# U half of the first projection as seven block products in batches 2 to 7, ahead of V, with the order drawn anew

## The chip, the cores and the metric

One Trainium2 chip, of which one core works. Its engines are TensorE (PE; the weight loads are shown as PEld), VectorE (DVE), ScalarE (ACT), GpSimd (POOL) and SyncE (SP, which here issues all DMAs). The metric is the device time of one execution in microseconds (us); lower is better.

## What is computed

Eight batches of 576 tokens. First attention: 8 heads of width 64, where heads 0 to 3 see a causal window of 32 tokens and heads 4 to 7 see every 32nd earlier token. Its output `x` (576 x 512 per batch) goes into a gated feed-forward block:

```
h = max(x @ w_in, 0);  u, v = h[:, :512], h[:, 512:]
v_n = (v - mean(v)) / sqrt(var(v) + 1e-6)          # over the 512 columns
v_s = w_spatial @ v_n + b_spatial[:, None]         # over the 576 tokens
out = (u * v_s) @ w_out
```

All is float32. A product of two float32 matrices is made as three matmuls in the format `float32r`: each operand is split into a high part and a rest, and high x high, high x rest and rest x high are added in PSUM.

## The kernel before

A batch's `x` lies transposed in four tiles `x[128 features, 2 parts, 576 tokens]`, one per pair of heads (`t` counts the pairs over all batches, four per batch; pairs 0 and 1 of a batch are local, 2 and 3 strided). Four stages follow each other on TensorE:

- **attention** of a pair: scores (L507 or L650), softmax on DVE, ACT and POOL, and the product with the values into PSUM `po` (L617 or L720). `evac_x` writes the high part of `x` (ACT, L434) and the rest (DVE, L422) straight from PSUM.
- **`moe_1`**: V, four tiles of 128 tokens, each 12 matmuls of 512 columns (L957), followed by relu out of PSUM (L915) and the normalisation (`chain`: L920 to L940) and the split into `vn` (L412 or L414, and L422). Then U, transposed, as eight groups of 12 matmuls of 288 columns (L999), each with a relu out of PSUM (ACT, L1013). The last 64 tokens of V are made in `moe_tail`, for two batches at once from batch 2 on.
- **`moe_2`**, first half: the product with `w_spatial` (L1079, and L1091 and L1092 for the tail and the bias), eight groups, each multiplied into `u` on DVE (L1101).
- **`moe_2`**, second half: the product with `w_out` (L1168), already as seven block products instead of eight (Strassen's scheme in Winograd's form): sums of blocks of `u*v_s` on DVE and POOL (`combine`, L825), splits (`parts`), and the blocks' results put together by DVE (`plus`, L1196) on their way out of PSUM. The output goes to HBM from the tiles `o` and `vv` (L1189).

Rings of buffers tie the stages: `r_x` (8 tiles of x), `r_vn` (one, used in turn for `vn` and for the sums of the second projection), `r_vv` (two, for V tiles and for the snapshots `s1` of the second projection), `r_g`, `r_u` (two each), `r_pm` (four PSUM banks).

The order of the work is set by a list scheduler, `Program.order`: every operation has a key (its priority), the engines that may do it with a price each, and its dependencies. It hands out operations engine by engine in modelled time; where two engines may do an operation, it takes the one that would end first by its prices. The keys come from the place of the stage (`plan`, `starts`, `due`) and from the table `KEYS`. Each engine then runs its instructions strictly in that order and waits with semaphores. `fillers` adds matmuls on zeros (L1349) where the schedule leaves TensorE idle early on.

## Time and profile before

| what | value |
|---|---|
| runs | 518.72 us median of 3 (517.84 to 520.33) |
| the profiled execution | 519.78 us, span 517.7 us |
| mean granted TensorE clock | 0.980 |
| busy: PE, DVE, ACT, POOL | 499.6, 363.0, 267.4, 129.0 us |
| U of one batch (L999), 96 matmuls | 12.79 us |
| longest wait of TensorE | 4.28 us, at 62.9 us, for `wsp_sb` |

The span runs from the first instruction to the last; the execution's own time is about 2 us longer. The four compute engines run side by side, so a busy engine matters only where another one waits for it. The page cuts the span into 40 slices of 12.9 us.

### The profile page before, as it was taken

Reading aid. Unit: us, or ns where it says so; the run is one execution under the profiler, and the core shown is the slowest. Engines: PE = TensorE matmul, PEld = TensorE weight load, DVE = VectorE, ACT = ScalarE, POOL = GpSimd, SP = SyncE. Lnnn points to the kernel's source line nnn. Section 1 sums busy time; section 2 is a strip of 40 time slices with the busy share of each in tenths; the row PEclk is TensorE's granted clock in tenths of the full one; section 3 lists DMA queues with packets and bytes.
Section 4 is the critical chain, followed back from the end, with each engine's and each line's share of the span. In section 5 each row is a group of like instructions: output and inputs, shape, how many; then the busy total and the mean of one; then the engine's idle time right before and its main releaser. Section 6 shows DMA issues by size and latency. Waiting matters only on the chain.

```text
span 517.7 us, 14663 instructions
## 1 busy us (share of the span) xinstructions
PE 499.6 (97%) x5884; PEld 459.3 (89%) x5884; DVE 363.0 (70%) x1093; ACT 267.4 (52%) x825; POOL 129.0 (25%) x245
## 2 busy tenths in 40 slices
PE   6779889999999999999999999999999999999997
PEld 3558779979999899998999899998999889998997
DVE  2899989969479747896369764897457861676156
ACT  5786765568554476456336276366446252233222
POOL 3355864043212121312102111233102120102000
PEclk9689979999999999999999999999999999999999
DMA  8897323454024322262023422063011300020002
GB/s 274 307 343 268 125 83 90 149 164 151 2 79 151 118 79 81 85 180 84 11 69 121 148 80 80 1 209 113 1 56 53 123 1 1 1 80 13 1 1 91
DMA packets 26243, 52.65 MB, mean 102 GB/s; under 512 B 3136, under 2 KB 11584, under 8 KB 26176
## 3 DMA queue, kind: packets, MB, share of 16 engines
q1 hardware_dynamic: 26176, 51.72, 30.3%
q8 instruction: 46, 0.75, 0.6%
q14 instruction: 21, 0.17, 0.1%
HBM read 42.27 MB, written 9.44 MB: 100 GB/s over the span
## 4 chain that ended last, share of the span: by engine, by line
PE 89%; DVE 4%; DMA 2%; ACT 2%; SPq 1%; POOL 1%; issue 1%; POOLq 0%
PE m L1079 20%; PE m L957 18%; PE m L1168 18%; PE m L999 18%; PE po L720 4%; PE po L617 3%; PE s L507 3%; PE s L650 2%; PE m L1091 2%; PE m L1092 2%; DMA k<-kT 1%; SPq L442 1%; DMA x<-wsp 1%; PE po L1349 1%; DVE w_in_sb L422 0%
## 5 line engine op out<-in xcount | busy, mean ns | idle before, releaser
L1079 PE MATMUL m<-wsp_sb,vn 128*128 128x288 f32 x768 | 113.3, 300 | 4.3 <-DVE wsp_sb L422 4.3
L1079 PEld LDWEIGHTS m<-wsp_sb,vn 128*128 128x128 f32 x768 | 107.3, 192 | 5.4 <-DVE wsp_sb L422 4.6
L999 PE MATMUL m<-x,w_in_sb 128*128 128x288 f32 x768 | 105.3, 297 | 0.0
L999 PEld LDWEIGHTS m<-x,w_in_sb 128*128 128x128 f32 x768 | 103.4, 188 | 1.2
L957 PE MATMUL m<-w_in_sb,x 128*128 128x512 f32 (+1 forms) x408 | 99.5, 399 | 0.0
L957 PEld LDWEIGHTS m<-w_in_sb,x 128*128 128x128 f32 (+1 forms) x408 | 74.5, 186 | 19.0 <-DVE x L422 0.2
L1168 PE MATMUL m<-g,w_out_sb 128*128 128x288 f32 x384 | 56.9, 298 | 0.0
L414 POOL TENSOR_SCALAR ptl<-pc 32x64 f32<-32x64 f32 (+3 forms) x89 | 37.9, 426 | 64.7 <-DVE pc L588 24.2
L1168 PEld LDWEIGHTS m<-g,w_out_sb 128*128 128x128 f32 x384 | 52.3, 188 | 1.0 <-ACT vv L434 0.3
L422 DVE TENSOR_TENSOR x<-po,x 128x288 fp32r<-128x288 f32 x64 | 27.6, 447 | 36.3 <-ACT x L434 35.6
L1101 DVE TENSOR_TENSOR u<-m,u 128x288 f32<-128x288 f32 x64 | 28.1, 453 | 30.9 <-PE m L1092 30.7
L564 ACT ACTIVATE pl<-pl,ml 128x64 f32<-128x64 f32 (+1 forms) x140 | 47.0, 339 | 4.7 <-DVE ml L544 4.3
L915 ACT ACTIVATE vv<-m 128x512 f32<-128x512 f32 (+1 forms) x37 | 22.0, 596 | 45.7 <-PE m L957 39.6
L412 ACT CAST g<-u 128x288 fp32r<-128x288 f32 x46 | 19.2, 434 | 50.2 <-DVE u L1101 49.0
L933 POOL TENSOR_TENSOR bn<-bn,sel 128x1 f32<-128x1 f32 (+1 forms) x37 | 21.1, 575 | 95.0 <-DVE bn L928 77.0
L1013 ACT ACTIVATE u<-m 128x288 f32<-128x288 f32 x64 | 25.7, 408 | 35.0 <-PE m L999 34.6
L1168 PE MATMUL m<-vn,w_out_sb 128*128 128x288 f32 x288 | 42.6, 297 | 0.0
L920 DVE BATCH_NORM_STATS2 bn<-vv 128x6 f32<-128x512 f32 (+1 forms) x37 | 25.3, 683 | 21.0 <-ACT vv L915 20.5
L1168 PEld LDWEIGHTS m<-vn,w_out_sb 128*128 128x128 f32 x288 | 39.5, 188 | 0.4
L434 ACT CAST x<-po 128x288 fp32r<-128x288 f32 x64 | 24.7, 397 | 26.2 <-PE po L617 14.4
L412 ACT COPY ptl<-pc 32x64 f32<-32x64 f32 (+3 forms) x103 | 35.7, 346 | 4.7 <-DVE pc L588 2.6
L422 DVE TENSOR_TENSOR g<-u,g 128x288 fp32r<-128x288 f32 x64 | 27.0, 449 | 7.9 <-ACT g L412 6.2
(131 smaller groups left out, 726.6 us busy)
## 6 DMA issues: line engine op xcount, KB each, us to landing
q<-qT SPq DMA_DIRECT2D x30, 295.0 KB, 4.2
outT<-o SPq DMA_DIRECT2D x48, 144.0 KB, 2.7
v_raw<-vs SPq DMA_DIRECT2D x13, 512.0 KB, 4.2
v_raw<-vl SPq DMA_DIRECT2D x16, 384.0 KB, 3.7
k<-kT SPq DMA_DIRECT2D x16, 304.0 KB, 4.5
kbd<-ks SPq DMA_DIRECT2D x32, 144.0 KB, 4.6
outT<-vv SPq DMA_DIRECT2D x16, 144.0 KB, 3.7
vn<-w_in SPq DMA_DIRECT2D x4, 512.0 KB, 4.5
```

The lines of the kernel that those rows point to most:

```text
L412: eng.copy(dst(), src())
L414: eng.tensor_scalar(dst(), src(), 1.0, 0.0, op0=ALU.mult, op1=ALU.add)
L422: eng.tensor_tensor(dst(), src(), f32(hi()), op=ALU.subtract)
L434: eng.copy(dst(), src())
L564: eng.activation(p_sb()[:m, u, :], src, AF.Exp, bias=st()[:m, u : u + 1], scale=SCALE if masked else -1.0, **total,)
L920: lambda eng: eng.bn_stats(bn()[:m, 0:6], v()[:m]), [(v,)], [(bn,)],
L957: eng.matmul(v_ps()[:m, :], x_at(kt)[:, a, :], w_in_sb[:, w, kt, HF:], start=(n == 0 and i == 0), stop=(n == NT - 1 and i == 2),)
L999: eng.matmul(u_ps()[:, :HS], w_in_sb[:, w, kt, f * P : (f + 1) * P], xs[NHP * b + kt]()[:, a, r], start=(n == 0 and i == 0), stop=(n == NT ...
L1013: lambda eng, u=u, f=f, u_ps=u_ps: eng.activation(u()[:, f * HS : (f + 1) * HS], u_ps()[:, :HS], AF.Relu),
L1079: eng.matmul(s_ps()[:, :HS], vn()[:, a, kt, fs], wsp_sb[:, w, kt, r], start=(kt == 0 and i == 0), stop=False,)
L1101: lambda eng, ug=ug, s_ps=s_ps: eng.tensor_tensor(ug(), s_ps()[:, :HS], ug(), op=ALU.mult),
L1168: eng.matmul(o_ps()[:, :HS], w_out_sb()[:, b_at, w, kk, a * P : (a + 1) * P], at(j, kk), start=first and kk == 0 and i == 0, stop=kk == 1 ...
```

## The change

**U in batches 2 to 7** (`moe_u`) is made as seven block products. `x` of a batch is cut in two halves of features (pairs 0 and 1, pairs 2 and 3) and two halves of tokens (288 each), the U half of `w_in` in 2 x 2 blocks of 256 x 256. Each product is 12 matmuls of 128 x 128 by 288 columns (two output tiles, two tiles of features, three matmuls for the parts), L1134 of the changed kernel. Before the products come four sums of x blocks (t1 to t4, two tiles each), made in place in float32, and their splits; four pieces are copied out of PSUM as snapshots or first results, and ten additions (L1145) put the rest together. The relu of U leaves the copy out of PSUM and goes into the multiplication by `v_s` (`scalar_tensor_tensor`, L1325).

**x** of these batches is written out of PSUM once, in float32 (`raws`), and split from there by `split_x`, over 576 columns. The `raws` stand in buffers that only the first batches use (`q1`, `k1`, halves of two `x1` tiles). `r_q`, `r_k`, `r_v` and `r_x` are each cut in two rings; from batch 2 on, one buffer of q, k and values and four x tiles are left.

**Sums of weights** (`block_weights`): s1 to s4 are made once after `moe_1` of batch 1, and stand in place of a block of `w_in` that is no longer read (s1), in `v_raw1` (s2) and in two `x1` tiles (s3, s4).

**Order**: in these batches U comes ahead of V in `moe_1`. The table `KEYS` has new numbers throughout, new keys for the first eight pairs' loads (`lq`, `lw`) and for the first memsets (`set`), and the filler's limits are in it (`w`).

```diff
-    "ls": (3541.9, 11770.0, 12130.5, 1637.8, 8461.5,),
+    "ls": (8504.2, 25952.5, 6448.5, 2672.9, 15921.1,),
+    "w": (65.6, 11.83, 0,),
-WARM_END, WARM_GAP, WARM_COST, WARM_COLS, WARM_SHARE = 110000.0, 700.0, 427.0, 256, 0.8
+U_COST = 11.2
+WARM_COST, WARM_COLS = 427.0, 256
...
-    r_q = Ring(sb, "q", [P, SP], F32, 2)
+    r_q = [Ring(sb, f"q{i}", [P, SP], F32, 1) for i in range(2)]
...
-    r_x = Ring(sb, "x", [P, 2, S], F32R, 8)
+    r_x = [Ring(sb, f"x{i}", [P, 2, S], F32R, NHP) for i in range(2)]
...
+    def split_x(t, due, x_t):
+        val, rin = raws[t], [(raws[t], c) for c in range(2)]
+        rnd(due - 0.7, S, lambda: x_t()[:, 0, :], val, rin, [(x_t, 0)])
+        rest(
+            due - 0.5, S, lambda: x_t()[:, 1, :], val, lambda: x_t()[:, 0, :],
+            [*rin, (x_t, 0)], [(x_t, 1)],
+        )
...
+    def block_weights(key):
+        n = HF // 2
+        for kk in range(2):
...
+                combine(at, n, made[name][1], in0, in1, op, reads, [tok(name)])
+            for name in ("s2", "s1", "s3", "s4"):
...
+                parts(at, n, made[name][1], dst, [tok(name)], to)
...
+    def moe_u(b, key):
+        side, more = r_vn.new(), r_g.new()
...
+        for kk in range(2):
+            lo, hi = xt(0, kk), xt(1, kk)
+            t1, t2, t3, t4 = col(lo, 0), col(hi, 1), col(lo, 1), col(hi, 0)
+            make(0, kk, t1, t3, t1, xin(lo), xin(lo)[:1])
+            make(2, kk, t3, t2, t3, xin(hi), xin(lo)[1:])
+            make(1, kk, t2, t2, t1, xin(lo)[:1], [*xin(hi), at_2])
+            make(3, kk, t4, t4, t2, [at_2, *xin(hi)], [at_4])
+            split(4, "t2", kk, t2, [at_2, *xin(hi)])
+            split(5, "t1", kk, t1, xin(lo)[:1])
+            split(6, "t3", kk, t3, xin(lo)[1:])
+            split(7, "t4", kk, t4, [at_4, *xin(hi)])
...
+        for a in range(2):
+            product("a11", (0, 0), alpha[a], a, t, True)
+            evac(t, HS, snap(a), lambda a=a: alpha[a]()[:, :HS], [(alpha[a],)], [(s1[a],)])
+        for a in range(2):
+            product("a12", (1, 0), alpha[a], a, t, False)
+            evac(t, HS, to(0, a), lambda a=a: alpha[a]()[:, :HS], [(alpha[a],)], [(uu[0], a)])
...
     def moe_1(b, key):
+        if b >= LEAD:
+            moe_u(b, key)
+            key += U_COST
...
+        if b >= LEAD:
+            return
         for hf in range(2):
             u = us[b, hf] = r_u.new()
...
+                    if b < LEAD:
+                        eng.tensor_tensor(ug(), s_ps()[:, :HS], ug(), op=ALU.mult)
+                    else:
+                        eng.scalar_tensor_tensor(
+                            ug(), ug(), 0.0, s_ps()[:, :HS], op0=ALU.max, op1=ALU.mult
+                        )
```

Three places of the built order follow. A row is one instruction or several equal ones (xN): line, operation, output <- inputs, shape of the output.

TensorE in the last batch, ahead of the product with `w_spatial`. Before, the last two of U's 32 rows (`m_6913`) stand ahead of it, and the last rows of V are 32 rows further up; `vn` is V normalised:

```order
L999 MATMUL m_6913<-x_6255,w_in_sb 128x288 x3
L999 MATMUL m_6913<-x_6399,w_in_sb 128x288 x3
L1079 MATMUL m_6927<-wsp_sb,vn_6761 128x288 x12
L1091 MATMUL m_6927<-wt_h,tail_6458 128x288
L1092 MATMUL m_6927<-wt_b,tail_b_74 128x288
```

In the change the last V tile (`m_7052`, L1022) stands there:

```order
L1022 MATMUL m_7052<-w_in_sb,x_26_6520 128x512 x3
L1300 MATMUL m_7070<-wsp_sb,vn_7035 128x288 x3
L1022 MATMUL m_7052<-w_in_sb,x_27_6530 128x512 x3
L1300 MATMUL m_7070<-wsp_sb,vn_7035 128x288 x3
L1300 MATMUL m_7085<-wsp_sb,vn_7035 128x288 x6
L1300 MATMUL m_7095<-wsp_sb,vn_7035 128x288 x6
L1300 MATMUL m_7103<-wsp_sb,vn_7035 128x288 x3
L1300 MATMUL m_7070<-wsp_sb,vn_7035 128x288 x3
L1300 MATMUL m_7085<-wsp_sb,vn_7035 128x288 x3
L1300 MATMUL m_7095<-wsp_sb,vn_7035 128x288 x3
L1300 MATMUL m_7103<-wsp_sb,vn_7035 128x288 x6
L1300 MATMUL m_7070<-wsp_sb,vn_7035 128x288 x3
```

U's 96 matmuls no longer stand between V and the product with `w_spatial`; the groups of that product are begun with the V tiles 0 to 2, in pieces of three, and the last row shown is the first that needs V tile 3.

TensorE in the change, from the end of the second projection of batch 6 (`m_6758` to `m_6813`, L1392) to U of batch 7 (`m_6879` and `m_6890` are a11 and a12 of the two output tiles, `m_6901` and `m_6910` s2*t2); before, V of batch 7 stood in place of the rows of L1134:

```order
L1392 MATMUL m_6777<-g_6762,w_out_sb_682 128x288 x6
L1392 MATMUL m_6813<-g_6785,w_out_sb_682 128x288 x6
L1134 MATMUL m_6879<-x_24_6505,w_in_sb 128x288 x3
L1134 MATMUL m_6879<-x_25_6512,w_in_sb 128x288 x3
L1134 MATMUL m_6890<-x_24_6505,w_in_sb 128x288 x3
L1134 MATMUL m_6890<-x_25_6512,w_in_sb 128x288 x3
L1134 MATMUL m_6901<-vn_6838,v_raw_2_1777 128x288 x6
L1134 MATMUL m_6910<-vn_6838,v_raw_2_1777 128x288 x6
L1134 MATMUL m_6879<-x_26_6520,w_in_sb 128x288 x3
L1134 MATMUL m_6879<-x_27_6530,w_in_sb 128x288 x3
L1134 MATMUL m_6890<-x_26_6520,w_in_sb 128x288 x3
```

The snapshots of `m_6879` and `m_6890` are copied to the tiles `vv` between their first and their last rows here, and the `vv` tiles are those from which the second projection's last results go to HBM.

VectorE in the first batch, up to the last rest of `w_spatial` (`wsp_sb`). Before:

```order
L544 ISA pl_75,ml_77<-s_779,cst_sb 64x64
L544 ISA ml_77 64x1
L422 TENSOR_TENSOR w_out_sb_822<-g_736,w_out_sb_822 128x256 x2
L422 TENSOR_TENSOR wsp_sb<-x_328,wsp_sb 128x576 x2
L422 TENSOR_TENSOR wsp_sb<-x_329,wsp_sb 128x576
```

In the change:

```order
L432 TENSOR_TENSOR w_out_sb_682<-g_620,w_out_sb_682 128x256
L432 TENSOR_TENSOR vn_761<-vv_833,vn_761 128x512
L513 RECIPROCAL mx_871<-mx_871 128x16
L432 TENSOR_TENSOR w_out_sb_682<-g_620,w_out_sb_682 128x256
L518 TENSOR_TENSOR pp_69<-pp_69,mx_871 128x16x18
L432 TENSOR_TENSOR wsp_sb<-x_0_546,wsp_sb 128x576
```

The masked maxima of a second local pair (ten L544 with their read-outs) no longer stand ahead of the last `wsp_sb`; 142 instructions of VectorE come up to it before, 123 in the change, and GpSimd makes two of the four rests of `w_spatial` instead of one.

More of the change, by code (lines that the diff above doesn't have):

```diff
@@ L34 @@
 SB = STRIDE // 4
+LEAD = 2
+ALONE = LEAD * NHP
 SP = S + STRIDE - RA
@@ L321, in fillers @@
         ends, free, found = {}, 0.0, {}
+        until, least, share = KEYS["w"]
         for at, n, e in issued:
@@ L761, in attention @@
                 load(
-                    due - 33, lambda j=j: kbd[j::2, t % 2, j, STRIDE:],
+                    first + 1, lambda j=j: kbd[j::2, t % 2, j, STRIDE:],
                     ks[b, hp - 2, j], [("k", t % 2, j)], 64 * S * 4, [("k0", t % 2)],
                 )
-            load(due - 20, v, vs[b, hp - 2], [(place,)], P * 1024 * 4)
+            load(last, v, vs[b, hp - 2], [(place,)], P * 1024 * 4)
             kin = [("k", t % 2, j) for j in range(2)]
-        xs[t] = r_x.new()
+        xs[t] = r_x[b if b < LEAD else 0].new()
+        if b >= LEAD:
+            raws[t] = raw_x(t)
         (local_attention if local else strided_attention)(t, due, q, k, v, [(place,)], kin)
+        if t in raws:
+            split_x(t, due, xs[t])
     def x_tok(t):
+        if t in raws:
+            return [(xs[t], i) for i in range(2)]
         return [(xs[t], i, c0) for i in range(2) for c0 in ((0, 3) if t % NHP < 2 else (0, 1))]
@@ L1024, in keep_tails @@
                 t = NHP * b + hp
+                if i == 1:
+                    at = lambda j, hp=hp: xt()[:, hp, j, TAIL:]
+                    src = lambda t=t: raws[t]()[:, 4 * P :]
+                    rin = [(raws[t], c) for c in range(2)]
+                    rnd(key, TAIL, lambda at=at: at(0), src, rin, [(xt, hp, 1, 0)], (POOL, ACT))
+                    rest(
+                        key, TAIL, lambda at=at: at(1), src, lambda at=at: at(0),
+                        [*rin, (xt, hp, 1, 0)], [(xt, hp, 1)],
+                    )
+                    continue
                 rnd(
@@ L1314, in attention_moe @@
         add(
-            -90, [(DVE, 250), (POOL, 400)],
+            KEYS["set"][1 + h], [(DVE, 250), (POOL, 260)],
             lambda eng, h=h: (
@@ L1344, in attention_moe @@
         (moe_tail, moe_1, moe_2)[kind](b, k0)
+        if kind == 1 and b == lead - 1 and nb > lead:
+            late.extend(raw_slots())
+            block_weights(k0 + cost[1])
     ctx.enter_context(tc.manual_schedule())
```

221 lines of the change are left out of this document (179 added, 42 removed), and 4 rows, old and new, of the table KEYS.

## Prediction

> **What bounds the kernel now.** I read the page first: busy times, slices, chain.
>
> ```profile
> span 517.7 us, 14663 instructions
> PE 499.6 (97%) x5884; PEld 459.3 (89%) x5884; DVE 363.0 (70%) x1093; ACT 267.4 (52%) x825; POOL 129.0 (25%) x245
> PE   6779889999999999999999999999999999999997
> PEclk9689979999999999999999999999999999999999
> PE 89%; DVE 4%; DMA 2%; ACT 2%; SPq 1%; POOL 1%; issue 1%; POOLq 0%
> ```
>
> TensorE carries the chain. Only the first six slices (78 us) hold digits below 9 and a lowered clock. The windows say how full the rest is, and what the other engines have left there:
>
> ```profile
> 70.00:130.00 60.00, 60.00 (x877) 55.02 (x877) 53.22 (x182) 38.83 (x130) 21.52 (x40) 0.98 0.39 120
> 170.00:290.00 120.00, 119.96 (x1519) 112.32 (x1520) 86.48 (x279) 63.42 (x206) 24.20 (x52) 1.00 0.32 99
> 100.00:510.00 410.00, 409.96 (x4664) 382.93 (x4663) 274.82 (x852) 200.15 (x624) 78.97 (x166) 1.00 0.24 76
> ```
>
> From 100 to 510 us TensorE is without work for 0.04 us. In the 120 us from 170, about the work of two batches, DVE has 33.5 us free, ACT 56.6 and POOL 95.8. So a matmul less is time less there, unless something new makes TensorE wait. The chain of waits gives the price of U, as the last batch shows:
>
> ```profile
> 464.16 11.20 PE m L957 x48
> 475.36 12.80 PE m L999 x96
> 488.15 1.58 PE m L1079 x12
> ```
>
> V, U and the product with w_spatial stand without a gap, and one matmul of U takes 12.80/96 = 133.3 ns. In the head, the timeline of TensorE:
>
> ```profile
> 62.64 0.29 PE L1079 MATMUL m<-wsp_sb,vn 128*128 128x288 f32 x1
> 67.21 7.99 PE L1079 MATMUL m<-wsp_sb,vn 128*128 128x288 f32 x42 [4.28 <-DVE wsp_sb L422]
> ```
>
> The load in the chain, and DVE's timeline:
>
> ```profile
> 53.05 4.08 DMA x<-wsp
> ```
>
> ```profile
> 63.92 0.21 DVE L544 CUSTOM_DVE_ANT_0 pl<-s,cst_sb 128x64 f32<-128x64 f32 x1
> ...
> 65.08 0.74 DVE L422 TENSOR_TENSOR w_out_sb<-g,w_out_sb 128x256 fp32r<-128x256 f32 x2
> 65.75 2.08 DVE L422 TENSOR_TENSOR wsp_sb<-x,wsp_sb 128x576 fp32r<-128x576 f32 x3
> ```
>
> The windows after the stop (PE busy, granted clock, DMA share):
>
> ```profile
> 67.20:72.00 4.80, 4.79 (x20) 0.50 0.29 107
> 72.00:77.00 5.00, 5.00 (x59) 0.99 0.02 5
> ```
>
> TensorE stands for 4.28 us, because the rests of w_spatial are last in a DVE queue: the load had landed by 57.13. After the stop it runs 4.80 us at a granted clock of 0.50, which costs another 2.4. This stop is worth 4.3 + 2.4 = 6.7 us.
>
> **The matmuls taken away.** Seven products of 12 instead of eight make 84 matmuls for 96, the same shape, in six batches: 72 x 133.3 ns = **-9.6 us**, all on the bounding engine. The chip cannot hide this term; only new waits can eat it.
>
> **The added elementwise work.** Its prices, from the groups by shape:
>
> ```profile
> L1013 ACT ACTIVATE u<-m 128x288 f32<-128x288 f32 x64 | 25.7, 408 | 35.0 <-PE m L999 34.6
> L434 ACT CAST x<-po 128x288 fp32r<-128x288 f32 x64 | 24.7, 397 | 26.2 <-PE po L617 14.4 <-PE po L720 9.9
> L422 DVE TENSOR_TENSOR x<-po,x 128x288 fp32r<-128x288 f32 x64 | 27.6, 447 | 36.3 <-ACT x L434 35.6
> L412 ACT CAST g<-u 128x288 fp32r<-128x288 f32 x46 | 19.2, 434 | 50.2 <-DVE u L1101 49.0 <-DVE o L825 0.4 <-DVE w_out_sb L422 0.2
> L422 DVE TENSOR_TENSOR g<-u,g 128x288 fp32r<-128x288 f32 x64 | 27.0, 449 | 7.9 <-ACT g L412 6.2 <-POOL g L414 1.7
> L825 DVE TENSOR_TENSOR u<-u,u 128x288 f32<-128x288 f32 x16 | 7.2, 456 | 0.5
> L1196 DVE TENSOR_TENSOR o<-m,o 128x288 f32<-128x288 f32 x32 | 14.4, 449 | 1.4 <-PE m L1168 1.3
> L412 ACT CAST wsp_sb<-x 128x576 fp32r<-128x576 f32 x1 | 0.7, 671 | 0.0
> L422 DVE TENSOR_TENSOR wsp_sb<-x,wsp_sb 128x576 fp32r<-128x576 f32 x3 | 2.1, 740 | 0.0
> L422 DVE TENSOR_TENSOR vn<-vv,vn 128x512 fp32r<-128x512 f32 x32 | 22.5, 717 | 3.0 <-ACT vn L412 2.0 <-POOL vn L414 0.5
> L422 DVE TENSOR_TENSOR w_in_sb<-vn,w_in_sb 128x512 fp32r<-128x512 f32 x4 | 4.3, 1084 | 0.0
> L422 POOL TENSOR_TENSOR w_out_sb<-g,w_out_sb 128x256 fp32r<-128x256 f32 x4 | 3.6, 899 | 0.2
> L422 POOL TENSOR_TENSOR wsp_sb<-x,wsp_sb 128x576 fp32r<-128x576 f32 x1 | 1.7, 1745 | 0.1
> ```
>
> Per batch it removes 8 relus (8 x 0.408 = 3.3 us) and 8 pairs that write x out of PSUM (8 x 0.844 = 6.8). It adds 8 plain copies of x (3.2), 4 splits of 576 columns (4 x 1.41 = 5.6), 8 sums (3.6), 8 splits of 288 (7.1), 4 copies and 10 additions out of PSUM (1.6 + 4.5). The net is 25.6 - 10.1 = 15.5 us of DVE-speed work per batch, 31 in 120 us, against the 186 us that the three engines have free. The multiplication by v_s keeps its shape and I price its new form at nothing (ends -0.1 and +0.1 us on DVE each, a tenth more or less of the 449 ns of L1196, which also reads PSUM, in a stage that DVE does not bound).
>
> The built order puts most of it on POOL: two-input operations on arrays with both inputs in SBUF go from 10 to 194 on POOL, from 289 to 257 on DVE. The rows 899 ns (256 columns) and 1745 (576) put one of 288 at about 0.98 us, an estimate, so POOL gains 184 x 0.98 = 180 us and stands near 309 of 509. All engines stay under three quarters; the average does not bind.
>
> **Do they get in each other's way?** The rests of 512 columns took DVE 717 ns for vn and 1084 for w_in_sb, in the head, where POOL is busy: half as much again. DVE's 257 operations, at 0.45 us, fill 23% of the time; 23% of POOL's 180 us is 41 us together, and half of it, 21 us, is DVE's loss. It fits in the free 33.5 of each 120; I charge TensorE **+1.5 us**, nearer to nothing since the row of 170 to 290 leaves room; the ends are 0 and +21 (every stretched operation waited for).
>
> The Trainium skill is harder here: on its page SBUF — State Buffer, section Who interferes with whom, a DVE instruction with two SBUF inputs and a GpSimd instruction that reads SBUF cannot run at once, and the later one blocks fully. The 1084 ns agree that one delays the other; no single row shows a full block. By that rule the whole 41 us would be lost to one of the two, an estimate that the third rival below turns into a time.
>
> **The sums of weights** are made once, between V of batch 1 and U of batch 2: 4 sums of 512 and 8 of 256 columns, 8 splits of 256, about 4 x 0.72 + 8 x 0.45 + 8 x 0.88 = 13.5 us. In 70 to 130 us DVE has 6.8 us free, ACT 21.2, POOL 38.5. They fit by sum, with DVE nearly full and POOL as the cover; I take **+1.0** (ends 0 and +6.7, half of them late).
>
> **U ahead of V.** Until now U's 12.8 us covered the last V tile's normalisation. Its length, in the last batch:
>
> ```profile
> 475.39 0.60 ACT L915 ACTIVATE vv<-m 128x512 f32<-128x512 f32 x1 [1.47 <-PE m L957]
> ```
>
> ```profile
> 479.55 0.69 DVE L422 TENSOR_TENSOR vn<-vv,vn 128x512 fp32r<-128x512 f32 x1 [0.69 <-ACT vn L412]
> ```
>
> From V's end at 475.36 to 480.24 are 4.9 us, plus a signal of some 0.2. In the built order 33 matmuls stand between V's last and the first that needs that tile: 4.4 us. So TensorE waits **0.7 us** in batch 7. In batches 3 and 5 attention matmuls of the next pair stand in the gap, and in 2, 4 and 6 the tail of V, so I take nothing there; the ends are 0 and, with one queued 1.7 us POOL operation in each of the three batches, +5.8.
>
> **The snapshots' buffers.** The tile vv that a second projection stores from is now written again by U's snapshot, 4 us earlier in need than by V:
>
> ```profile
> 464.29 0.67 SPq L1189 DMA_DIRECT2D outT<-vv  x1
> ```
>
> ```profile
> outT<-vv SPq DMA_DIRECT2D x16, 144.0 KB, 3.7
> ```
>
> The last store, issued 0.1 us after the projection's end (464.16), lands by the median of 3.7 us (the issue table's last number) 3.8 after it; the copy (0.4) and a signal end at 4.4, and a12 of the second tile stands at 30 matmuls, 4.0. That is 0.4 us at worst, six times 2.4; **+0.5**, because in batches with attention its matmuls stand between.
>
> **The head.** Ahead of the last rest of w_spatial DVE has 19 instructions less: ten masked maxima (63.92 to 65.08: 1.2 us), two rests of w_in (2.2), one each of vn, wsp_sb and a sum, against some 2.5 us of others. That is about 3 us less, and POOL has two more array operations of w_in and one of w_spatial. At the same place TensorE has 1.8 us more attention to do first. Together they exceed 4.28, so the stop should close and with it the half clock: up to -6.7. Against it: POOL's rest of 1745 ns can be the last one now, and the filler matmuls are gone. I take **-4.0**, the stop without the clock; ends 0 and -6.7. Loads keep their number and bytes, and the one q and k buffer from batch 2 on costs nothing while DMA is 24% busy from 100 us.
>
> **Sum:** -9.6 + 1.5 + 1.0 + 0.7 + 0.5 - 4.0 = -9.9 us. The profiled execution took 519.78 (span 517.7): 509.9. The median of the runs is 1.06 lower: **508.8 us**.
>
> **Rivals.**
> - The head does not gain: the stop goes to another wait, a sum or a rest on POOL. DVE's last rests depend on POOL's high parts. 508.8 + 4.0 = 512.8.
> - Everything is covered and the head gains in full: 518.7 - 9.6 - 6.7 = 502.4. For it: 0.04 us of waiting in 410 now. Against it: two new waits with less cover.
> - The lock: POOL and DVE block each other and the sums reach U late. If a quarter of the 41 us reaches TensorE in place of the 1.5, 508.8 + 8.8 = 517.6, no change that can be told. For it the 1084 ns; against it that V and the product stages leave time.
> - Slower: the hand-over from V to w_spatial in batches 3, 5 and 7. If queued work makes the last tile's chain 4.3 us longer than its cover, each wait is like the one at 62.9: 4.3 and then 2.4 of half clock. That is 3 x 6.7 = 20 less the 0.7 counted: 528. It needs ten masks (1.2), a POOL operation (1.7) and 0.9 more ahead of it in all three, and batch 7 has no attention.
>
> **Chances.** Forecast 45%, head without gain 20%, all covered 15%, lock 13%, hand-over 7%. The range 502 to 517 holds the first three and some of the lock, and cuts off most of the rest. A measurement here tells about 0.5% (2.6 us) from no change. Faster than 516.1: the first three and a little of the lock, 82%; within: most of the lock, 11%; slower than 521.3: 7%.
>
> **What would show it.** 84 matmuls of 133 ns per U, 11.2 us, in place of 12.8; TensorE without a stop of 4 us before the first w_spatial product and a clock above 0.98; waits under 1 us between V and w_spatial in batch 7 and at a12; POOL near 310 us busy and DVE near 370. Wrong would be TensorE under 99% busy from 100 us on, a group of stops behind POOL, or a clock of 0.5 after 80 us.

## The result and the profile after

The changed kernel takes **546.89 us** (median of 4 runs, 545.78 to 547.54), the kernel before 518.85 (517.84 to 520.33, on the same chip): a ratio of **1.054, 95% interval 1.051 to 1.057**. It is 28 us slower, where 508.8 was forecast. The profiled execution has a span of 545.3 us. Its busy times, slices, granted clock and chain of waits:

```profile
span 545.3 us, 14749 instructions
...
PE 494.4 (91%) x5790; PEld 450.8 (83%) x5790; DVE 416.1 (76%) x1073; ACT 290.3 (53%) x886; POOL 295.6 (54%) x424
...
PE   3397969999899899999999999998998999899997
...
PEclk9989999999989999999999999999999999999999
...
PE 39%; DVE 36%; ACT 7%; DMA 7%; POOL 5%; issue 4%; SPq 1%; DVEq 0%; ACTq 0%; POOLq 0%
```

TensorE held 89% of the chain before; now VectorE holds nearly as much as TensorE. The clock is not the reason: its mean over the span is 0.991, before 0.980. To see where the time went, both runs are cut at the same two places of the work: the start of the last matmul with `wt_b` that closes the `w_spatial` stage of batch 1, and the one of batch 7. From the timeline of TensorE, before:

```profile
152.51 0.29 PE L1092 MATMUL m<-wt_b,tail_b 97*128 97x288 f32 x1
...
502.73 0.29 PE L1092 MATMUL m<-wt_b,tail_b 97*128 97x288 f32 x1
```

and after:

```profile
68.41 5.46 PE L1300 MATMUL m<-wsp_sb,vn 128*128 128x288 f32 x39
78.03 0.40 PE L1312 MATMUL m<-wt_h,tail 128*128 128x288 f32 x1 [4.16 <-DVE tail L432]
...
160.20 0.29 PE L1313 MATMUL m<-wt_b,tail_b 97*128 97x288 f32 x1
...
529.56 0.29 PE L1313 MATMUL m<-wt_b,tail_b 97*128 97x288 f32 x1
```

| stretch, us | before | after | difference |
|---|---|---|---|
| up to the last matmul of the product with `w_spatial` in batch 1 | 152.51 | 160.20 | +7.7 |
| from there to the same place in batch 7 (the six changed batches) | 350.22 | 369.36 | +19.1 |
| the rest | 14.97 | 15.74 | +0.8 |

The middle stretch should have shrunk by 9.6 us to 340.6, so 28.7 us of waiting and of broken-up work came in there. The windows of the middle stretch, and of some stages in it, before (the stretch; V and U of batch 3; its product with `w_spatial`; the second projections of batches 3 and 4 with the attention beside them):

```profile
152.64:502.86 350.22, 350.18 (x3855) 328.54 (x3853) 231.06 (x695) 161.89 (x493) 63.37 (x132) 1.00 0.22 72
237.00:257.80 20.80, 20.80 (x226) 19.30 (x225) 10.09 (x23) 9.95 (x23) 5.49 (x11) 1.00 0.01 1
257.80:272.80 15.00, 15.00 (x118) 14.99 (x113) 9.97 (x41) 4.97 (x25) 0.43 (x1) 1.00 0.22 69
272.80:288.60 15.80, 15.76 (x263) 14.82 (x262) 14.82 (x40) 10.00 (x27) 4.17 (x11) 1.00 0.52 171
336.40:352.00 15.60, 15.60 (x294) 14.89 (x281) 15.53 (x48) 9.78 (x32) 4.62 (x11) 1.00 0.59 193
```

and after (the stretch; V of batch 3; its product with `w_spatial`, now with attention beside it; the second projection of batch 4):

```profile
160.33:529.69 369.36, 348.86 (x3718) 319.09 (x3717) 281.27 (x696) 178.49 (x534) 186.29 (x268) 1.00 0.22 69
256.50:267.00 10.50, 10.50 (x47) 8.49 (x46) 5.27 (x13) 2.94 (x5) 2.75 (x5) 1.00 0.01 2
267.00:287.50 20.50, 20.38 (x309) 19.14 (x308) 19.76 (x56) 15.01 (x50) 16.82 (x22) 1.00 0.34 100
352.20:368.00 15.80, 14.86 (x270) 13.66 (x268) 14.83 (x27) 8.32 (x24) 11.57 (x16) 1.00 0.29 100
```

TensorE now stands 20.5 us of the stretch (369.36 - 348.86), in 32 stops of 0.2 to 1.9 us. The other 8.2 of the 28.7 us are longer rows. Most of them are an after-effect of the stops, by this estimate: a matmul of 288 columns has a row of 297 ns, and the next one starts 133 ns after it where the run is unbroken, so at each stop the last row runs out alone, 32 x 0.16 = 5.2 us. The third column of busy times is VectorE. Over the stretch it is busy 76%, which looks harmless; but it is 50% busy beside V (5.27 of 10.50) and 96% beside `w_spatial` and the attention that now stands there (19.76 of 20.50; 66% before, without attention). The stage of the second projection was 94 and nearly 100% full in the kernel before (14.82 of 15.80 and 15.53 of 15.60), rows that the prediction did not read; TensorE lost 0.04 us beside them. What TensorE waits for, and what the two-input operations cost, by groups (the last column is the idle time ahead and who ended it):

```profile
L1300 PE MATMUL m<-wsp_sb,vn 128*128 128x288 f32 x768 | 117.4, 303 | 4.5 <-DVE vn L432 2.2 <-DVE u L1325 0.9 <-ACT vn L422 0.9
L1392 PE MATMUL m<-vn,w_out_sb 128*128 128x288 f32 x288 | 43.7, 300 | 4.5 <-DVE vn L432 2.4 <-DVE o L1420 2.0
L1134 PE MATMUL m<-x,w_in_sb 128*128 128x288 f32 x144 | 23.6, 305 | 6.4 <-ACT vv L444 3.8 <-DVE vv L1420 2.6
L1134 PE MATMUL m<-vn,x 128*128 128x288 f32 x72 | 11.5, 295 | 0.0
L1312 PE MATMUL m<-wt_h,tail 128*128 128x288 f32 x64 | 19.2, 307 | 7.4 <-DVE tail L432 7.4
L432 DVE TENSOR_TENSOR x<-x,x 128x576 fp32r<-128x576 f32 x17 | 19.2, 1158 | 0.0
L432 DVE TENSOR_TENSOR g<-u,g 128x288 fp32r<-128x288 f32 x29 | 21.2, 746 | 0.3 <-POOL g L424 0.3
L432 POOL TENSOR_TENSOR g<-u,g 128x288 fp32r<-128x288 f32 x35 | 31.7, 912 | 14.6 <-ACT g L422 13.5 <-PE m L1392 0.5
```

A matmul of U costs what it did (295 ns against 297; 305 in the group that holds the stops). Of the 20.1 us in the 32 stops, 6.8 stand at U (snapshots and last results in `vv`), 5.6 at `w_spatial` and its tail (splits `vn`), 5.0 at the second projection (splits `vn`, sums `o`) and 2.7 at attention, in three waits for a load of values (1.02, 0.94 and 0.76 us). Two chains behind the stops at U, first a queue of VectorE and the stop that it ends, then a copy of ScalarE that waits for a store and the longest stop:

```profile
174.69 0.84 DVE L432 TENSOR_TENSOR vn<-q,vn 128x288 fp32r<-128x288 f32 x1
175.45 2.04 DVE L432 TENSOR_TENSOR vn<-x,vn 128x288 fp32r<-128x288 f32 x2
...
177.78 0.44 DVE L1420 TENSOR_TENSOR vv<-m,vv 128x288 f32<-128x288 f32 x1
178.27 1.85 PE L1134 MATMUL m<-x,w_in_sb 128*128 128x288 f32 x12 [0.94 <-DVE vv L1420]
...
375.99 0.40 ACT L444 COPY vv<-m 128x288 f32<-128x288 f32 x1 [1.55 <-DMA outT<-vv]
376.44 1.05 PE L1134 MATMUL m<-x,w_in_sb 128*128 128x288 f32 x6 [1.92 <-ACT vv L444]
```

In the first, three splits of the new sums (read from `q1` and an `x1` tile) stand ahead of the second projection's result in `vv`. In the second, the snapshot may not be written to `vv` until the store from it has landed. A rest of 288 columns takes VectorE 746 ns, before 449; one of 576 columns 1158, before 740.

### The profile page after: what moved, and what is told of

Its sections match the earlier page's. It is cut to its first block, busy times and chain, and to the rows that moved or that the text cites. A ratio compares the mean times of both kernels' runs of the same rounds, so it can differ in the third digit from the quotient of the medians.

```text
span 545.3 us, 14749 instructions
## 1 busy us (share of the span) xinstructions
PE 494.4 (91%) x5790; PEld 450.8 (83%) x5790; DVE 416.1 (76%) x1073; ACT 290.3 (53%) x886; POOL 295.6 (54%) x424
## 4 chain that ended last, share of the span: by engine, by line
PE 39%; DVE 36%; ACT 7%; DMA 7%; POOL 5%; issue 4%; SPq 1%; DVEq 0%; ACTq 0%; POOLq 0%
PE m L1022 11%; PE m L1134 8%; DVE vn L432 7%; PE m L1300 6%; PE m L1392 5%; DVE x L432 4%; ACT pl L613 3%; PE m L1210 2%; DMA outT<-vv 2%; DVE bn L985 2%; DVE vv L1005 2%; DVE o L1420 2%; DVE g L432 2%; PE po L666 2%; DMA v_raw<-vs 2%
## 5 line engine op out<-in xcount | busy, mean ns | idle before, releaser
L1300 PE MATMUL m<-wsp_sb,vn 128*128 128x288 f32 x768 | 117.4, 303 | 4.5 <-DVE vn L432 2.2
L1022 PE MATMUL m<-w_in_sb,x 128*128 128x512 f32 (+1 forms) x408 | 100.2, 400 | 0.0
L1022 PEld LDWEIGHTS m<-w_in_sb,x 128*128 128x128 f32 (+1 forms) x408 | 75.2, 187 | 18.9 <-issue 0.2
L1392 PE MATMUL m<-g,w_out_sb 128*128 128x288 f32 x384 | 57.4, 298 | 1.2 <-ACT vv L444 1.1
L1392 PEld LDWEIGHTS m<-g,w_out_sb 128*128 128x128 f32 x384 | 52.7, 188 | 2.9 <-ACT vv L444 2.2
L424 POOL TENSOR_SCALAR ptl<-pc 32x320 f32<-32x320 f32 (+3 forms) x81 | 34.9, 431 | 30.3 <-DVE pc L637 20.7
L1392 PE MATMUL m<-vn,w_out_sb 128*128 128x288 f32 x288 | 43.7, 300 | 4.5 <-DVE vn L432 2.4
L422 ACT COPY ptl<-pc 32x320 f32<-32x320 f32 (+3 forms) x111 | 38.8, 350 | 11.7 <-DVE pc L637 10.4
L1392 PEld LDWEIGHTS m<-vn,w_out_sb 128*128 128x128 f32 x288 | 39.4, 188 | 6.7 <-DVE vn L432 2.9
L985 DVE BATCH_NORM_STATS2 bn<-vv 128x6 f32<-128x512 f32 (+1 forms) x37 | 25.4, 688 | 21.7 <-ACT vv L980 21.6
L432 POOL TENSOR_TENSOR g<-u,g 128x288 fp32r<-128x288 f32 x35 | 31.7, 912 | 14.6 <-ACT g L422 13.5
L1005 DVE TENSOR_SCALAR vv<-vv,bn 128x512 f32<-128x512 f32 (+1 forms) x37 | 24.8, 670 | 14.3 <-POOL bn L998 14.3
L422 ACT CAST g<-u 128x288 fp32r<-128x288 f32 x55 | 22.5, 434 | 16.2 <-DVE u L1325 10.5
L1145 DVE TENSOR_TENSOR u<-m,vv 128x288 f32<-128x288 f32 x36 | 16.2, 451 | 19.4 <-PE m L1134 16.2
L1134 PE MATMUL m<-x,w_in_sb 128*128 128x288 f32 x144 | 23.6, 305 | 6.4 <-ACT vv L444 3.8
L1325 DVE SCALAR_TENSOR_TENSOR u<-u,m 128x288 f32<-128x288 f32 x48 | 20.3, 442 | 10.1 <-PE m L1313 10.0
L1134 PEld LDWEIGHTS m<-x,w_in_sb 128*128 128x128 f32 x144 | 19.8, 188 | 8.8 <-ACT vv L444 5.0
L1210 PE MATMUL m<-x,w_in_sb 128*128 128x288 f32 x192 | 26.5, 297 | 0.0
```

Of the source, the lines that this page charges most:

```text
L422: eng.copy(dst(), src())
L424: eng.tensor_scalar(dst(), src(), 1.0, 0.0, op0=ALU.mult, op1=ALU.add)
L432: eng.tensor_tensor(dst(), src(), f32(hi()), op=ALU.subtract)
L985: lambda eng: eng.bn_stats(bn()[:m, 0:6], v()[:m]), [(v,)], [(bn,)],
L1005: lambda eng: eng.tensor_scalar(v()[:m], v()[:m], bn()[:m, 6:7], bn()[:m, 9:10], op0=ALU.subtract, op1=ALU.mult),
L1022: eng.matmul(v_ps()[:m, :], x_at(kt)[:, a, :], w_in_sb[:, w, kt, HF:], start=(n == 0 and i == 0), stop=(n == NT - 1 and i == 2),)
```

## The experiments

The theories: **A**, the two-input work on GpSimd; **B/H**, the new place and hand-overs of U; **C**, VectorE has no room; **D**, the new table of keys; **E**, the fewer buffers; **F/G**, attention pressed into the late stages, or not; **I**, the sums of x and their splits. Each time stands beside the kernel before on the same chip, with the ratio and its 95% interval.

### Two-input work back on VectorE

One number of the table moves 185 operations:

```diff
-    "dp": (18607.0, 455.0,),
+    "dp": (18607.0, -1038.4,),
```

> The changed kernel with one number of the order's table set back: the surcharge that the planner puts on VectorE for an operation with two inputs that GpSimd could also do (dp, second number) is -1038.4 ns as before, not +455. It moves about 185 two-input operations from GpSimd to VectorE (TENSOR_TENSOR: VectorE 431 to 616, GpSimd 229 to 44); products, buffers and all other keys stay. Theory A (the lost time comes from two-input work on GpSimd, which is itself slow, 0.9 to 1.7 us, and stretches VectorE's operations): TensorE's waits fall from 47 us towards 25, the rest of vn out of u falls from 847 back to about 490 ns, and the time goes to 515 to 528 us. Theory B (the waits belong to the new place of U and its buffers, whoever does the sums): within 1.5% of 547. Theory C (VectorE has no room for that work): VectorE above 430 us busy and the time 540 or more.

Measured: **549.9 us, ratio 1.059 (1.057 to 1.062)**, no gain.

```profile
PE 496.8 (91%) x5790; PEld 454.4 (83%) x5790; DVE 434.1 (79%) x1258; ACT 272.4 (50%) x832; POOL 154.0 (28%) x293
```

GpSimd falls from 296 to 154 us, and the time does not fall with it. The middle stretch is 364.0 us, 5 better than the change, and the head 7.5 worse (batch 1 ends at 167.65). So A is not the main cause; what is taken from GpSimd fills VectorE instead (434.1 us), and both the time and VectorE lie where C put them.

### The kernel before with its work moved to GpSimd

```diff
-    "dp": (12894.8, -1038.4,),
+    "dp": (12894.8, 455.0,),
...
-    "dpt": (657.16,),
+    "dpt": (887.79,),
```

> The kernel before with that surcharge as in the change (455 ns, for the first 888 us): 109 two-input operations go from VectorE to GpSimd (TENSOR_TENSOR: VectorE 499 to 390, GpSimd 45 to 154), nothing else is changed on purpose. Theory A: slower than before by 10 to 25 us (109 of 185 moved operations, and the changed kernel lost some 37 us against its own sum), with TensorE waits after 100 us where there was 0.04. Theory B: 517 to 523 us.

Measured: **527.8 us, ratio 1.017 (1.015 to 1.020)**. Moving 109 operations to GpSimd costs 8.4 us, below A's 10 to 25, and nothing like the change's distance from its forecast, 38 us. Of the 8.4, 4.2 lie ahead of batch 2 (batch 1 ends at 156.68) and 2.1 in the middle stretch (352.3).

### The disputed price by itself

Streams of ten, each begun when the ones before are done:

```
        ("a", (("vector", tt),)),
        ("b", (("gpsimd", tt),)),
        ("c", (("vector", tt), ("gpsimd", tt))),
        ("e", (("vector", from_psum), ("gpsimd", tt))),
        ("h", (("vector", one), ("gpsimd", tt))),
```

> Not the computation: streams of ten equal operations on 128 x 288 float32, on one engine alone and on two at once, and zeros as output. It measures the disputed price: a two-input operation on VectorE (alone about 0.37 to 0.45 us) and one on GpSimd (alone 0.6 to 0.9 us), and both at once. If the two exclude each other fully, both streams at once take the sum of their lone times (about 1.3 us per pair); if they only slow each other, VectorE's takes up to 0.85 and GpSimd's stays near 0.95. With one input from PSUM, or with one input in all, VectorE should be untouched if only the second SBUF input matters.

Groups of the run: v is VectorE, g GpSimd; a and b are two-input operations alone, c both at once, d VectorE with one input from PSUM alone and e beside GpSimd, g a one-input operation of VectorE alone and h beside GpSimd.

```profile
L35 POOL TENSOR_TENSOR gc<-x,go_c 128x288 f32<-128x288 f32 x10 | 9.8, 1010 | 0.5 <-ACT go_c L70 0.5
L35 DVE TENSOR_TENSOR vc<-x,go_c 128x288 f32<-128x288 f32 x10 | 9.2, 985 | 8.6 <-ACT go_c L70 8.6
L44 DVE TENSOR_SCALAR vh<-go_h 128x288 f32<-128x288 f32 x10 | 7.6, 834 | 0.5 <-ACT go_h L70 0.5
L35 POOL TENSOR_TENSOR gb<-x,go_b 128x288 f32<-128x288 f32 x10 | 7.5, 794 | 9.4 <-ACT go_b L70 9.4
L38 DVE TENSOR_TENSOR ve<-bank,go_e 128x288 f32<-128x288 f32 x10 | 3.7, 450 | 0.5 <-ACT go_e L70 0.5
L38 DVE TENSOR_TENSOR vd<-bank,go_d 128x288 f32<-128x288 f32 x10 | 3.7, 448 | 1.1 <-ACT go_d L70 1.1
L35 DVE TENSOR_TENSOR va<-x,go_a 128x288 f32<-128x288 f32 x10 | 3.7, 447 | 0.0
L44 DVE TENSOR_SCALAR vg<-go_g 128x288 f32<-128x288 f32 x10 | 2.3, 304 | 4.3 <-ACT go_g L70 4.3
```

This is one execution. Ten of each take 3.7 and 7.5 us alone, 11.2 one after the other, and 9.8 together: of the 3.7 us that could overlap, 1.4 do. The slow-down is larger than the milder expectation (985 ns, not up to 850). One input from PSUM leaves VectorE untouched (448 and 450 ns). The Trainium skill, page "SBUF — State Buffer", section "Who interferes with whom", says that the two share one pair of ports that an instruction holds to its end; the 9.8 of 11.2 us nearly agree.

### The old U with the new keys and buffers

`moe_1` and `moe_2` as before, with no `raws`, no `moe_u` and no `block_weights`, under the table of keys and the rings of the change:

```diff
-        if b >= LEAD:
-            raws[t] = raw_x(t)
...
-        if b >= LEAD:
-            moe_u(b, key)
-            key += U_COST
```

> The changed kernel with its table of keys and its split rings, but U in the old form in all batches: eight products behind V, x written out of PSUM in two parts, no sums of x or of weights. 159 TENSOR_TENSOR are on GpSimd, 385 on VectorE. Theory A: slower than before, 528 to 540 us, since the sums of the second projection and the rests are still on GpSimd. Theory B (the new U costs the time): 519 to 525 us. Theory D (the new table of keys is bad by itself, above all in the head): 540 or more, most of the loss before 100 us.

Measured: **555.8 us, ratio 1.073 (1.066 to 1.081)**. The form without the seven products is 8.9 us slower than the change. B falls as the only cause: keys and rings lose the time even with the old U. D has the size right and the place wrong: 4.5 us of the loss lie ahead of batch 2 (batch 1 ends at 156.98) and 28.0 in the middle stretch (378.3).

### Rings alone, keys alone

The kernel before with the rings of the change, and then with its own rings and the new keys:

```diff
-    r_x = Ring(sb, "x", [P, 2, S], F32R, 8)
+    r_x = [Ring(sb, f"x{i}", [P, 2, S], F32R, NHP) for i in range(2)]
```

(and the same for q, k and values.)

> The kernel before, table of keys and all, with only the rings of the change: one q, one k and one value buffer from batch 2 on instead of two, four x tiles instead of eight; U in eight products behind V, nothing on GpSimd that was not there (TENSOR_TENSOR: VectorE 499, GpSimd 45, as before). Theory E (the four x tiles and single load buffers make attention wait for V and U of the batch before, and then TensorE wait for attention): 535 to 560 us, with waits at the attention matmuls (for loads of q, k, v or for the rests of x). Theory D (the new keys cost the time): 517 to 524 us. Theory A (GpSimd) says 517 to 524 as well, but the first four runs already spoke against it as the main cause.

> The kernel before, with its rings of two and of eight, U in eight products behind V, and only the new table of keys. Theory D: 540 us or more. Theory E: 520 to 532 us, of which up to 8.4 by the work that the new keys give to GpSimd (163 TENSOR_TENSOR; the kernel before with 154 there took 8.4 us more).

> The changed kernel, seven products ahead of V, with the table of keys of before for everything that both have (TENSOR_TENSOR: VectorE 610, GpSimd 50). Theory D: 505 to 520 us, the 9.6 us of matmuls less than before and some waits at U. Theory E: 535 to 555 us, since the buffers are those of the change.

| us | keys of before | keys of the change |
|---|---|---|
| rings of before, old U | 519.3 | 534.4, ratio 1.030 (1.028 to 1.033) |
| rings of the change, old U | 563.6, ratio 1.086 (1.082 to 1.090) | 555.8 |
| rings of the change, new U | 554.1, ratio 1.068 (1.062 to 1.074) | 546.9 |

The rings alone cost 44 us, a little more than E's range, the new keys alone 15, between the ranges of D and E, and the new U gives 9 us back in both columns. Of the keys' 15 us, 12 lie ahead of batch 2 (batch 1 ends at 164.63); the middle stretch is 350.6, as before. Of the rings' 44, the stretch up to batch 1 takes 13.4 and the middle one 32.6.

### Which rings

> The kernel before with one ring of the change: x in two rings of four tiles, of which only the first is used from batch 2 on; q, k and values keep two buffers, U stays in eight products, the keys are those of before. Theory E1 (the four x tiles are the cause: the attention of the next batch can write x only after the last product of this batch that reads it): 540 to 565 us. Theory E2 (the single load buffers are the cause): 517 to 525 us.

> The kernel before with the other rings of the change: one q, one k and one value buffer from batch 2 on, eight x tiles as before. Theory E2: 535 to 555 us, with waits of TensorE for loads of q and values. Theory E1: 518 to 530 us; some waits for loads can be there, but attention runs far enough ahead to take them.

Measured: x alone **533.8 us (1.027, 1.022 to 1.031)**, loads alone **532.9 (1.026, 1.022 to 1.029)**; neither expectation of "the one or the other" holds. The x ring costs 13.5 us in the middle stretch (363.7) and nothing in the head. The load rings cost 12.6 us in the head and 0.9 behind it (351.1). Both together cost 32.6 there: of 22.0 us of stops, 14.7 stand at attention's matmuls, 5.0 of these behind a load of q or values; with the x ring alone it was 2.1 of 7.3. That fits attention that is held back by x and has nothing fetched ahead with which to catch up. A part is the clock: behind stops the granted clock is 0.59 from 209 to 217 us in the run with the x ring (worth 3.3 us), and in the run with both 0.66 from 228 to 238, 0.57 from 366 to 370 and 0.72 from 488 to 494 (worth 6.8); in the kernel before it was 1.00 throughout the stretch. The head of the run with the load rings, where before there was no stop between 47.5 and 62.9 us:

```profile
60.94 1.19 PE L702 MATMUL s<-kbd,q 128*32 128x36 f32 x64 [7.30 <-DVE ml L593]
...
69.72 0.84 PE L1203 MATMUL m<-x,w_in_sb 128*128 128x288 f32 x2 [2.09 <-ACT w_in_sb L422]
```

Its first 100 us issue the same kinds of loads in another order. One buffer less between two requests may change what the scheduler finds ready, so that a table of keys made for one order does not fit the next; no run here shows that this is the reason.

### The new U in fewer batches

```diff
+BLOCK = 6
-        if b >= LEAD:
+        if b >= BLOCK:
             raws[t] = raw_x(t)
...
-        xs[t] = r_x[b if b < LEAD else 0].new()
+        xs[t] = r_x[b % 2 if b < BLOCK else 0].new()
```

> The new U and the new rings only in batches 6 and 7 (eight x tiles, two q, k and value buffers up to batch 5), keys of before; the sums of weights are made after V of batch 5. If the loss belongs to the buffers, it scales with the batches that run with few of them: of the some 35 to 44 us of six batches a third at most, and batch 7 has no attention behind it, so 518 to 530 us; the matmuls give back 2 x 1.6 = 3.2 us. If the new U itself (place ahead of V, snapshots, sums) costs the time, the same range holds and the waits stand at its matmuls, not at attention's.

> The same with batches 4 to 7: the loss of the buffers in three attention stages (batches 4 to 7) instead of five, 525 to 545 us, less 4 x 1.6 = 6.4 us of matmuls already in that range; linear between the two-batch and the six-batch form (554).

Measured: **543.9 us (1.047, 1.042 to 1.051)** and **547.8 (1.054, 1.050 to 1.059)**: above both ranges, and not in proportion to the batches. 19 to 20 us of it are lost up to the end of batch 0, in the head again (the product with `w_spatial` of batch 0 ends at 105 to 106 us, before 86); batches 2 to 5 of the two-batch form take what they took before, and batches 6 and 7 take 6.5 us more, in spite of 3.2 us of matmuls less.

### Attention earlier, VectorE only later, load buffers back

```diff
-    "lead": (-4.89,),
+    "lead": (10.0,),
...
+    "dp2": (12894.8, -1038.4,),
...
-            held = KEYS["dp"][locks] if now < KEYS["dpt"][0] * 1000.0 else 0.0
+            held = KEYS["dp" if now < 200000.0 else "dp2"][locks] if now < KEYS["dpt"][0] * 1000.0 else 0.0
...
-    r_q = [Ring(sb, f"q{i}", [P, SP], F32, 1) for i in range(2)]
+    r_q = [Ring(sb, "q", [P, SP], F32, 2)] * 2
...
+            name: (x_homes[1], lambda t: t.rearrange("p a s -> p (a s)")) for name in ("s2", "s3", "s4")
```

> The changed kernel with one number of the table of keys set anew: from batch 2 on attention falls due 14.9 us earlier (lead -4.89 to 10). In the built order more of attention then stands beside V and U (348 matmuls behind a V row for 196) and less in the second projection. Theory F (the buffers press the next batch's attention into the stages of w_spatial and w_out, where VectorE is then 95% busy and its sums come late): 530 to 541 us, less waiting from 160 us on. Theory G (attention cannot go earlier whatever its key, since the buffers hold it, or the sums of U are late by themselves): 544 to 552 us.

> The changed kernel with the two-input work given back to VectorE only behind 200 us of the planner's time (surcharge -1038.4 ns there, +455 ahead of it, so that the head stays as it is): 114 operations leave GpSimd. By the stage times of the first experiment (batches 3 to 7: 293 us against 301 with GpSimd) theory A in its small form says 8 us less than the change, 537 to 541 us. If that difference came from the shifted head alone, 545 to 549.

> Both numbers together. If F and A are two causes beside each other, 522 to 534 us; if both are the same full VectorE queue, no better than the better one of the two alone.

> The changed kernel with two q, k and value buffers kept in all batches. Room for them is made by leaving work out: the sums of weights s2, s3 and s4 share one tile, so their products take the same, wrong block; every instruction, its shape and its engine choice stay possible as they were. Theory E (x tiles and load buffers together hold attention): the loss behind the head falls from 34 us by about half, as in the form with the x ring alone (18.6 us lost there against 38.5 with both): 525 to 537 us. Theory G or A: 543 to 550 us.

| run | us | ratio (95%) | middle stretch |
|---|---|---|---|
| the change | 546.9 | 1.054 (1.051 to 1.057) | 369.4 |
| attention earlier | 555.4 | 1.071 (1.066 to 1.075) | 372.4 |
| VectorE only behind 200 us | 547.5 | 1.056 (1.052 to 1.061) | 370.3 |
| both | 549.7 | 1.059 (1.053 to 1.064) | 367.5 |
| two load buffers | 558.6 | 1.076 (1.066 to 1.081) | 365.7 |

None brings a gain. The earlier attention and the two load buffers end above every range given for them. VectorE behind 200 us lies in the range for a difference that came from the shifted head alone (545 to 549), and both together are no better than the better one, as the second reading says. But the 5 us of the first experiment may only be hidden here: behind stops the granted clock fell to 0.66 from 245 to 250 us and from 405 to 410 and to 0.72 from 462 to 468, worth 5.1 us, where the changed kernel kept 1.00 in the whole stretch. The two-buffer form gains 3.7 us in the stretch and loses 15 in the head. So neither the due time of attention nor the engine of the sums nor the load buffers, set anew by itself under these keys, wins the time back.

### The products alone, with the sums, with the buffers

The kernel before with its keys, and `moe_u` without sums (plain halves of x and blocks of `w_in` go into the products):

```diff
+        plain = {"t1": (0, 1), "t2": (1, 1), "t3": (0, 0), "t4": (1, 0)}
...
+                half, hf = plain.get(src, src)
```

With the sums, `moe_u` makes and splits them from x, into a ring of their own:

```diff
+        made, side, more = r_sum.new(), r_vn.new(), r_g.new()
...
+            make(0, kk, col(lo, 1), col(lo, 0), x_tok(lo))
```

With the few buffers, the changed kernel loses its sums:

```diff
-            block_weights(k0 + cost[1])
```

> The kernel before, with its keys and its buffers (eight x tiles, two q, k and value buffers), and of the change only the products: in batches 2 to 7 U is made ahead of V as seven block products with snapshots, four copies and ten additions. Left out are the sums of x and of weights: the products that need them read plain halves of x and plain blocks of w_in, so U is wrong. It costs nothing to have x written in two parts as before. Theory H (U ahead of V, its snapshots and additions cause the waits): a loss behind the head of 20 us or more, as in all forms with the new U so far (31 to 44), so 520 to 535 us. Theory E (few buffers and the sums that fill them): a loss like that of before (5 us) or up to 10, so 509 to 515 us, near the prediction without its gain in the head.

> The products alone (517.5 us) and beside them the eight sums of x per batch and their splits into vn and g, as in the change, with eight x tiles and two q, k and value buffers as before. Left out are the sums of weights (plain blocks of w_in in their place), x is summed by its high part, and s1 to s4 of w_out share one place, which makes room for the sums: U and the output are wrong, the work is there. The sums bring 8 x 0.45 + 8 x 0.88 = 10.7 us of VectorE-speed work per batch. Theory I (the sums and splits are the cause: they fill VectorE in the stages of w_spatial and w_out and use the one vn buffer twice): 530 to 545 us, waits at the sums of the second projection and at U. Theory E (few buffers): 517 to 524 us.

> The products with the buffers of the change (four x tiles, one q, k and value buffer from batch 2 on, x written once in float32 and split later), but without the sums of x and of weights (plain halves and blocks in their place, so U is wrong). Keys as in the run with the changed kernel and the old table (554.1 us), which had both, and whose head was 13 us longer than before by the load buffers. Theory E: 545 to 554 us, a loss behind the head of 25 to 34 us. Theory I: 525 to 534 us, of which some 13 in the head, and behind it at most 10 more than the products alone.

Measured: products alone **517.5 us (0.995, 0.993 to 0.997)**; with the sums **528.5 (1.017, 1.012 to 1.022)**; with the few buffers **532.4 (1.025, 1.022 to 1.028)**. The first two lie between the ranges of their two theories, the third in that of I. With the changed kernel under the old keys (554.1) they make a square: the sums cost 11.0 us with the buffers of before and 21.7 with the few. TensorE's ends of the stretch and some of its stops, products alone, with the copy of ScalarE that ends one of them:

```profile
152.90 0.29 PE L1276 MATMUL m<-wt_b,tail_b 97*128 97x288 f32 x1
...
172.63 2.67 PE L1097 MATMUL m<-x,w_in_sb 128*128 128x288 f32 x18 [0.99 <-ACT vv L444]
...
233.71 0.40 ACT L444 COPY vv<-m 128x288 f32<-128x288 f32 x1 [1.29 <-DMA outT<-vv]
234.16 6.12 PE L1097 MATMUL m<-x,w_in_sb 128*128 128x288 f32 x44 [0.84 <-ACT vv L444]
...
500.56 0.29 PE L1276 MATMUL m<-wt_b,tail_b 97*128 97x288 f32 x1
```

with the sums, with VectorE's queue ahead of one of the stops, and the later part of the second projection of batch 3 with the first 3 us of the next U (windows):

```profile
155.82 0.30 PE L1308 MATMUL m<-wt_b,tail_b 97*128 97x288 f32 x1
...
291.02 3.12 DVE L433 TENSOR_TENSOR vn<-sum,vn 128x288 fp32r<-128x288 f32 x5
294.06 0.45 DVE L1415 TENSOR_TENSOR o<-m,o 128x288 f32<-128x288 f32 x1
294.56 2.66 PE L1387 MATMUL m<-g,w_out_sb 128*128 128x288 f32 x18 [1.21 <-DVE o L1415]
...
512.18 0.29 PE L1308 MATMUL m<-wt_b,tail_b 97*128 97x288 f32 x1
```

```profile
282.80:300.00 17.20, 15.02 (x197) 13.99 (x196) 17.06 (x47) 7.93 (x26) 5.24 (x9) 1.00 0.58 191
```

with the few buffers, and then with both (the changed kernel, keys of before):

```profile
162.93 0.29 PE L1278 MATMUL m<-wt_b,tail_b 97*128 97x288 f32 x1
...
515.00 0.29 PE L1278 MATMUL m<-wt_b,tail_b 97*128 97x288 f32 x1
```

```profile
169.12 0.29 PE L1313 MATMUL m<-wt_b,tail_b 97*128 97x288 f32 x1
...
534.92 0.29 PE L1313 MATMUL m<-wt_b,tail_b 97*128 97x288 f32 x1
```

The stretch takes 347.7, 356.4, 352.1 and 365.8 us. So the way from 350.2 to the changed kernel's 369.4 goes: matmuls -9.6 (worked out); waits at the hand-overs of the products +7.0 (347.7 against 340.6); sums of x with their splits +8.7; few buffers, with x written once and split from there, +4.4; both together 5.0 more than their sum, the sums of weights in it; the new keys, GpSimd's work with them, +3.6. These are stage times of one profiled execution each, and the runs of one kernel lie up to 4.4 us from their median, so a term may be off by about that much: the 8.7 and the 7.0 stand clear of it, the other three hardly. And 1.7 of the 5.0 are the clock: the run with both stops for 2.54 us at 283.2 for a load of values, and its granted clock is 0.72 from 286 to 292, while it is 1.00 in the stretch of the other runs of this list.

In the window with the sums VectorE is busy 17.06 of 17.20 us and TensorE 15.02. In the second projection of batch 3 before, VectorE was busy 14.82 of 15.80 and TensorE 15.76; with the products alone (274 to 291 us) 16.50 of 17.00 and 16.24. So the stage had about 1 us to spare, and the splits of the sums go into it: five of them, 3.1 us, stand in VectorE's queue ahead of the result `o` for which TensorE stops at 294.56, and the same five ahead of the stops of 2.10 us at 417.35 and 1.62 at 473.51. A full VectorE does not stop TensorE by itself (15.53 of 15.60 us before, and no stop); what stands ahead of a result that TensorE needs does.

## Why the prediction was wrong

By the two profiled executions the change came out 27.6 us longer where the sum said 9.9 shorter. The 37.5 us between them are 11.7 in the head, 7.2 for the sums and splits, 5.8 for U's hand-overs, 4.4 for the few buffers, 4.0 for these together with the sums (the sums of weights in it), 3.6 for the keys in the middle stretch and 0.8 behind it. The step that failed is the one that let all new work and all waits pass nearly free: room was read off an average, and the buffers and the order drawn anew got no price.

- **The matmuls, -9.6 us:** agrees. With the same keys and rings the new U is 8.9 us faster than the old one, under the old keys 9.5 (563.6 to 554.1), and a matmul of U takes 295 ns against 297. "Only new waits can eat it" is what came.
- **The added elementwise work, +1.5 with ends 0 and +21:** mis-sized, by its room. "It fits in the free 33.5 of each 120" took the average of two batches for the room of each stage. The sums and splits cost 8.7 us on top of the products, inside the ends but far from the 1.5, and more beside the few buffers. "The average does not bind" was true and beside the point: VectorE was 94 to nearly 100% busy in the stage that had to take the splits, and 49% beside V and U (10.09 of 20.80), and the splits stand ahead of results that TensorE waits for.
- **GpSimd and VectorE in each other's way:** the collision is there, and harder than the half that was assumed (9.8 us for 11.2 us of work). But putting the work back on VectorE gained nothing, which fits one shortage of both engines better than a price of GpSimd alone. POOL was forecast near 310 us busy and came to 296; DVE near 370 and came to 416, with the rests of 288 columns at 746 ns.
- **U ahead of V, +0.7, and the snapshots' buffers, +0.5:** 7.0 in the products alone. The hand-over from V to `w_spatial` in batch 7 was there and smaller than worked out, a stop of 0.20 us for 0.7 (the 0.2 for a signal has no row; from `o`'s end at 294.51 to TensorE's start at 294.56 it is 0.05). The snapshots were sized too low: stops behind `vv` of 3.15 us in all, at the place and from the store that were named; the working had 0.4 us in a batch at worst and let attention's matmuls take most of it, and single stops reach 0.99. Of the rest, two stops of 0.7 us stand behind the sums `o`, and 2.2 us are no stop: TensorE's rows of the stretch add up to 342.9 us where 340.6 were due. By the estimate above, 1.3 of these are the last rows that run out alone at the eight stops.
- **Buffers:** put at nothing, without a price. The prediction gave the q and k buffers nothing, since "DMA is 24% busy", and gave no price at all to the four x tiles. The share of DMA time does not tell how early a load may start: it was 0.22 in the stretch before and after, and now TensorE waits 2.7 us there for loads of values. Behind the head the load rings alone are indeed nearly free (0.9 us), but the x ring costs 13.5 and both 32.6 with the old U (3.3 and 6.8 of these by the clock); in the new form, where x lands in float32 first, few buffers cost 4.4 alone.
- **The head, -4.0:** +7.7 up to batch 1. The stop ahead of `w_spatial` closed, as worked out (68.41 without a wait), and 10 us later one of 4.16 us stands at the tail: the first rival named that. What it missed is that an order drawn anew is a risk of its own: the new keys alone made batch 1 end 12.1 us later.
- **The sums of weights, +1.0:** not measured apart.
- **The signs:** two of the three signs of being wrong came: TensorE is busy 416.7 of 440 us from 100 us on (95%), and the granted clock is 0.50 from 151 to 154 us, behind a stop of 1.98 us at the tail of batch 1. The third did not: no stop of the middle stretch ends behind POOL.
- **The rivals:** none was it. The lock, weighed with 8.8 us, pointed the right way. The slower case had its 20 us in the wrong place: the stops at `w_spatial` and its tail stay at 1.1 us or less in the six batches.

What stays open is why few buffers and sums together cost more than apart (5.0 us, 3.3 without the clock, hardly clear of the noise), why the load rings and the keys disturb the head, and why neither an earlier due time of attention nor more load buffers helped the changed kernel. Attention's matmuls stood to 48% beside V and U before and to 14% in the change (23.0 of 47.5 and 6.6 of 46.2 us of TensorE rows behind 110 us), which fits a crowding of its work into the late stages, but moving it ahead made the run slower. Whether x tiles as many as before would cure it was not tried in the changed kernel, where the other four hold `raws` and sums of weights. No version here beats the kernel before with the full computation; the products alone are 0.5% faster and leave the sums out.
